# Attention, a routed expert layer and a second MLP on one core: a kernel's scheduler plans several times, with deadlines found backwards

## The chip, the core and the metric

The kernel runs on one core of one Trainium2 chip. The metric is the device time of one execution in microseconds (us), the median of several runs. The core has five engines with a queue each: TensorE (PE in the profile), VectorE (DVE), ScalarE (ACT), GpSimd (POOL) and SyncE (SP). SP issues most of the loads.

## The reference

Three layers follow one another. All inputs are float32.

```
scores = scale * q @ k^T             # B=4, H=8, S=576, D=64
scores = where(block_i >= block_j, scores, -1e9)      # blocks of 64
attn   = softmax(scores) @ v
x      = attn as [2304, 512]
...
logits = normalise(x) @ normalise(expert_emb)^T / tau   # 8 experts
e      = argmax(logits); gate_w = softmax(logits)[e]
x2[t]  = gate_w[t] * (relu(x[t] @ w1[e]) @ w2[e])     # 512 -> 1024 -> 512
...
h      = x2 @ w_in                                    # 512 -> 2048
out    = (h * sigmoid(h)) @ w_out                     # 2048 -> 512
```

## The kernel before

**Three stages.** Attention goes over 16 pairs (a batch and two heads). For each pair TensorE makes scores, DVE their row maxima, ACT the exponentials p, TensorE turns p by a matmul with the identity (pt) and multiplies it by v. Two things lie beside attention: the conversion of the second MLP's weights, and, as soon as the first 13 columns of 128 tokens are done, the routing of those tokens.

The expert layer goes over tiles of 128 tokens. A tile `s` holds tokens of one expert: its rows are gathered, turned (xt, L1297), multiplied by w1 (h, `first` L1315), sent through relu (L1331), turned again (ht, L1338), multiplied by w2 (y, `second` L1354) and scaled by the gate value (`yout`, L1377). There are 20 such tiles, and code behind a branch (`further`, L1524) for the case that more are needed.

The second MLP goes over chunks of three tiles: yt turns the rows, g multiplies by w_in, the silu follows (sg), o multiplies by w_out (`chunk`, L1390). Tiles and chunks are interleaved, so that the chunks give TensorE work from tile 3 on.

**Precision.** A product is made of three matmuls on a high and a low part of each operand. So weights are split on the way: ACT or DVE makes the high part (a CAST, w1s or w2s or w), DVE the low part (a subtraction). For the first tiles some of the four parts of the inner dimension are left whole and go through a plain float32 matmul: `DIRECT = (2, 1, 1, 1)` parts of tiles 0 to 3 (L47). The weights w_in and w_out arrive in a bit format that `_Convert` (L474) mends: 32 pieces of 512 KB (16 of w_in, 16 of w_out), each with one load, two ACT instructions and three or four of DVE. The last addition of pieces 0 to 11 is made on POOL, that of the rest on DVE. `CONV_AT` (L1610) says which of attention's pairs takes a piece along: 1 to 12. The other pieces follow between the tiles (`conv.more`).

**Who sets the order.** Nothing is written in its final order by hand. `_Plan` (L83) records every operation as an item: the engines that can do it, a cost in ns, what it depends on, and a rank, which is its place in the program plus a shift. `issue` (L350) then goes through time: at each step the engine that can begin first takes, among its items that are ready, the one with the smallest rank; a change of TensorE between float32 and float32r counts as 30 ranks (`STAY`). Where an item can go on two engines, the planner takes the one on which it ends sooner. A load's cost is its bytes at 360 B/ns (180 for runs under 512 bytes). What comes out are five fixed queues. The planner's costs decide only the order; on the chip each engine waits for what it really needs.

**Routing** is in three parts. `early` (L1089) finds the tokens of tiles 0 to 5 from the first 13 columns. `late` (L1121) chooses the experts of the other columns, and finds places and tokens (r_rows, r_tok_rhs and the tok matmuls) of tiles 6 on and the table of experts (esi). `rest` (L1144) makes the gate values (g1 for tiles 0 to 5, g2 for the rest). The squares of x, which the gate values need, are made by ACT at the end of attention (L869) into a ring of three PSUM buffers that attention's pt matmuls also use.

**Loads of weights.** `weights` (L1212) loads parts of an expert's w1 and w2 into wraw, a buffer that holds one expert; `begin` (L1242) starts the first tile's, in the order 0, 1, 2, 3.

All of it is recorded by one helper, so nearly every row of the profile has the line L192; rows are told apart by tile names. The functions that the change touches, and those that call them, are these:

Of the kernel before, what the change touches and what calls it, by code (L numbers as in the profile page):

```python
# [9 lines left out]
F32 = mybir.dt.float32  # L10
# [34 lines left out]
BG, WC, LM = 1, 2.4, 0.0  # L45
SM, CVS, SPS, ES = 0, 0, 40, 0
# [4 lines left out]
EARLY1, EARLY = 11, 26  # L51
# [7 lines left out]
STAY, CHANGE = 30, 190.0  # L59
SQS = 100  # L60
LS = -1000
# [21 lines left out]
class _Plan:  # L83
# [13 lines left out]
    class _Pool:  # L97
        def __init__(self, plan, pool, bufs):
            self.plan, self.pool, self.bufs = plan, pool, bufs
            self.names, self.done = [], set()  # L100
# [5 lines left out]
        def tile(self, shape, dt, tag=None, name=None, bufs=None):  # L106
# [5 lines left out]
            if tag is not None:  # L112
                ring = self.plan.rings.setdefault((id(self), tag), [])
# [8 lines left out]
    def __init__(self, tc):  # L122
        self.nc = tc.nc
        for e in self.ENGINES:
            setattr(self, e, self._Engine(self, e))
        self.rings, self.before, self.seen, self.users = {}, {}, {}, {}
# [8 lines left out]
        self.even = BW  # L135

# [62 lines left out]
    def call(self, alts, ins, outs, table=None, lead=0.0, dma=False):  # L199
# [3 lines left out]
        last = self.items[-1] if n and self.end[-1] is None else None  # L203
        pe = alts.get("tensor")
        if (pe and last is not None and "tensor" in last["alts"]
                and last["out"] == outs[0][0] and last["prio"] == n - 1 + self.shift
# [5 lines left out]
        else:  # L212
            it = dict(alts=alts, out=outs[0][0], deps=set(), table=table, lead=lead, dma=dma,
                      prio=n + self.shift, margin=self.margin if pe else 0.0)
# [77 lines left out]
    def _cost(self, engine, method, args, kw):  # L292
# [12 lines left out]
        if method == "dma_start":  # L305
# [4 lines left out]
            return n * mybir.dt.size(out.dtype) / (360.0 if run >= 512 else 180.0)  # L310
# [39 lines left out]
    def issue(self, ahead=100.0, until=()):  # L350


        items, free = self.items, self.free
        new = [n for n, end in enumerate(self.end) if end is None]
# [37 lines left out]
        while until:  # L392
            t, e = min((max(free[e], min(ready[n] for _, n in w)), e)
                       for e, w in waiting.items() if w)

            prio, n = min((x for x in waiting[e] if ready[x[1]] <= t + ahead),
                          key=lambda x: (x[0] + STAY * self._changes(e, items[x[1]]), x[1]))
# [21 lines left out]
            if it["dma"]:  # L419
# [6 lines left out]
                end = self.dma + 1150.0  # L426
# [23 lines left out]
    QUEUE = 1500.0  # L450

# [72 lines left out]
def _attention(first, ctx, late, tc, plan, q, k, v, emb, tau, x_dram, identr, lr_all, ss_all, conv=None):  # L524
# [85 lines left out]
    rmat = cp.tile([P, NPAIR, 2, D + E], F32, name="rmat")  # L610

# [201 lines left out]
    def e_units(i):  # L813
# [110 lines left out]
class _Route:  # L924
# [196 lines left out]
    def late(self, pool, psum):  # L1121
# [3 lines left out]
        self.choose(pool, NC1, NT)  # L1125
# [18 lines left out]
    def rest(self, pool, psum):  # L1144
# [24 lines left out]
        V.tensor_tensor(self.cpos[:, NE:], cp, dif, ALU.add)  # L1169


# [18 lines left out]
        for name, (rows, cols), m, s0 in (("g1", self.first, NC1, 0),  # L1190
                                          ("g2", self.second, NT, NE)):
            pt = self.invert(pool, psum, name, rows, cols, g3[:, 0:m])
            g = self.gate[:, s0:s0 + cols.shape[2]]
            V.tensor_copy(g, pt[:, 0])
            V.tensor_tensor(g, g, pt[:, 1], ALU.add)
            V.tensor_tensor(g, g, pt[:, 2], ALU.add)


def _layers(ctx, stage, early, scores, late, tc, plan, w1, w2, x_dram, y_dram, out, ident, route, xgs, conv, right):
# [12 lines left out]
    def weights(s, i, n, keep):  # L1212
# [4 lines left out]
        def f(eng):  # L1217
# [7 lines left out]
            else:  # L1225
# [7 lines left out]
                  [plan._box(wraw[:, i:i + n])], lead=1100.0 + 1000.0 * new, dma=True)  # L1233
# [8 lines left out]
    def begin(s, n=KC):  # L1242
        for i in range(0, 2 * KC, n):
            weights(s, i, n, False)
# [52 lines left out]
    def xt(s):  # L1297
        xg = XT[s]
        pt = psum(f"xt_{s}")
# [6 lines left out]
        ps["t"].close(pt)  # L1306
# [8 lines left out]
    def first(s, kc):  # L1315
        if kc == 0:
            HS[s] = [psum(f"h{n}_{s}") for n in range(2)]
        k = slice(kc * P, kc * P + P)
        if kc < direct(s):
            for n in range(2):  # L1320
                nc.tensor.matmul(HS[s][n], WH[s, "x"][:, k],
                                 wraw[:, kc, 512 * n:512 * n + 512], start=(kc == 0), stop=False)
# [3 lines left out]
        xh, xl = (XT[s][:, a, k] for a in range(2))  # L1326
        for n in range(2):
            c = slice(512 * n, 512 * n + 512)
            three(HS[s][n], xh, xl, hi[:, 0, c], lo[:, 0, c], kc == 0, kc == KC - 1)

    def relu(s):  # L1331
        h = htp.tile([P, FF], F32, tag="h", name=f"h_{s}")
        for n in range(2):
# [4 lines left out]
    def ht(s, n):  # L1338
        if n == 0:
            HT[s] = htp.tile([P, 2, FF], F32R, tag="ht", name=f"ht_{s}")  # L1340
        pt = psum(f"ht{n}_{s}")
# [8 lines left out]
        ps["t"].close(pt)  # L1350
# [3 lines left out]
    def second(s, i):  # L1354
        if i == 0:
            YP[s] = psum(f"y_{s}")
# [377 lines left out]
```

## Time and profile before

| | |
|---|---|
| runs | 911.73, 913.6, 916.29 us; median 913.6 us |
| the profiled execution | 912.01 us, span 910.3 us |
| granted TensorE clock, mean | 0.992 |
| instructions in the span | 13872 |

The profile is one execution on the chip. PE is TensorE's matmuls, PEld its weight loads, SPq is SP's queue. "Busy" leaves out waits on semaphores. An arrow `<-` after a duration in brackets names what ended the wait before the row's instruction; an `<-` between names stands between what is written and what is read. PEclk is the granted clock as a share of 2.4 GHz.

### The profile page before, as it was taken

To read this page: it belongs to the slowest core of one execution; us is meant where nothing else is said; L and a number is where in the kernel's file an instruction comes from. 1 tells how busy PE (TensorE), PEld (TensorE's weight loads), DVE (VectorE), ACT (ScalarE), POOL (GpSimd) and SP (SyncE) were. 2 spreads that over 40 slices of the span, in tenths; PEclk is the share of its full clock that TensorE was granted. 3 is DMA by queue.
4 is the path that set the end of the run, shared out by engine and by line. 5 is a ranking of instruction groups with operands and counts; after the bars stand their busy time and mean duration, and the time that the engine had idled before them with its cause. 6 is when DMAs were issued, how large, how long until landed. Compare 5 with 4: busy or idle time off the path is not lost.

```text
span 910.3 us, 13872 instructions
## 1 busy us (share of the span) xinstructions
PE 861.3 (95%) x4986; PEld 714.7 (79%) x4986; DVE 720.4 (79%) x1249; ACT 564.7 (62%) x1147; POOL 116.7 (13%) x158
## 2 busy tenths in 40 slices
PE   5999999987899989999999999999999999999995
PEld 4777677655567878887888888888898998898894
DVE  5889899776889979999788888888667667666672
ACT  6888787766468658879766566676334334334332
POOL 2112121224100000012311110031001001001001
PEclk9999999999899999999999999999999999999998
DMA  5436353352133338751200322143102002000000
GB/s 186 138 114 173 104 180 97 76 208 64 62 139 133 131 106 281 269 185 42 71 24 24 116 68 72 58 139 105 58 1 70 1 1 70 1 0 36 1 1 35
DMA packets 38441, 82.77 MB, mean 91 GB/s; under 512 B 5208, under 2 KB 13400, under 8 KB 38368
## 3 DMA queue, kind: packets, MB, share of 16 engines
q1 hardware_dynamic: 32736, 63.47, 21.1%
q0 software_dynamic: 5632, 18.36, 6.5%
q8 instruction: 41, 0.67, 0.3%
q14 instruction: 32, 0.26, 0.1%
HBM read 123.23 MB, written 13.11 MB: 150 GB/s over the span
## 4 chain that ended last, share of the span: by engine, by line
PE 61%; issue 0%; DVE 0%; ACT 0%; POOL 0%; POOLq 0%; ACTq 0%
PE o L192 20%; PE g L192 20%; PE y L192 9%; PE h L192 9%; PE ht L192 1%; PE yt L192 1%; PE xt L192 1%; POOL out_dram L1465 0%; ACT ys L192 0%; POOLq L1729 0%; DVE sg L192 0%; DVE ht L192 0%; ACT sg L192 0%; DVE yt L192 0%; DVE xt L192 0%
## 5 line engine op out<-in xcount | busy, mean ns | idle before, releaser
L192 PE MATMUL o<-w,g 128*128 128x512 f32 x864 | 228.5, 396 | 0.0
L192 PE MATMUL g<-yt,w 128*128 128x384 f32 x1152 | 227.5, 338 | 0.2 <-issue 0.2
L192 PEld LDWEIGHTS g<-yt,w 128*128 128x128 f32 x1152 | 203.2, 188 | 13.5 <-issue 0.5
L192 PEld LDWEIGHTS o<-w,g 128*128 128x128 f32 x864 | 160.5, 188 | 30.4 <-DVE g L192 0.7
L192 ACT ACTIVATE sg<-g 128x384 f32<-128x384 f32 x96 | 47.3, 493 | 136.2 <-PE g L192 135.6
L192 PE MATMUL y<-w2s,ht 128*128 128x512 f32 x450 | 128.8, 400 | 0.7 <-DVE w2s L192 0.7
L192 PE MATMUL h<-w1s,xt 128*128 128x512 f32 x450 | 112.3, 400 | 0.7 <-ACT xt L192 0.5
L192 DVE TENSOR_TENSOR w1s<-wraw,w1s 128x1024 fp32r<-128x1024 f32 x75 | 91.4, 1222 | 18.6 <-ACT w1s L192 18.0
L192 PEld LDWEIGHTS h<-w1s,xt 128*128 128x128 f32 x450 | 84.5, 189 | 22.0 <-issue 2.7
L192 DVE TENSOR_TENSOR w2s<-wraw,w2s 128x1024 fp32r<-128x1024 f32 x75 | 91.2, 1223 | 11.9 <-ACT w2s L192 10.0
L192 PEld LDWEIGHTS y<-w2s,ht 128*128 128x128 f32 x450 | 81.1, 188 | 13.7 <-DVE w2s L192 1.0
L192 ACT ACTIVATE p<-s,mx 128x576 f32<-128x576 f32 (+4 forms) x160 | 82.1, 524 | 12.6 <-DVE mx L192 12.0
L192 ACT CAST w2s<-wraw 128x1024 fp32r<-128x1024 f32 x67 | 70.6, 1054 | 23.4 <-PE y L192 8.3
L192 DVE TENSOR_REDUCE mx<-s 128x1 f32<-128x576 f32 (+2 forms) x96 | 64.8, 705 | 17.1 <-PE s L250 16.7
L192 DVE TENSOR_TENSOR w<-win,w 128x512 fp32r<-128x512 f32 x96 | 65.8, 688 | 15.8 <-ACT w L192 15.6
L192 ACT CAST g<-sg 128x384 fp32r<-128x384 f32 x96 | 49.3, 515 | 43.9 <-DVE sg L192 42.4
L192 ACT CAST w1s<-wraw 128x1024 fp32r<-128x1024 f32 x59 | 62.3, 1058 | 21.0 <-PE y L192 10.0
L250 PE MATMUL s<-ks,qs 64*128 64x288 f32 (+4 forms) x576 | 60.0, 341 | 12.8 <-ACT p L192 6.4
L192 DVE TENSOR_TENSOR w<-wout,w 128x512 fp32r<-128x512 f32 x96 | 65.6, 684 | 1.8 <-ACT w L192 1.6
L192 ACT CAST w<-win 128x512 fp32r<-128x512 f32 x87 | 54.0, 623 | 19.8 <-PE o L192 19.5
L192 PE MATMUL pt<-ident,p 128*128 128x128 f32 (+1 forms) x400 | 60.4, 287 | 5.8 <-ACT p L192 2.2
L250 PEld LDWEIGHTS s<-ks,qs 64*128 64x128 f32 x576 | 46.5, 198 | 18.9 <-ACT p L192 9.3
(192 smaller groups left out, 1110.5 us busy)
## 6 DMA issues: line engine op xcount, KB each, us to landing
wraw<-in_moe_w_dram SPq DMA_DIRECT2D x76, 1024.0 KB
wbits<-in_moe_w_in_dram SPq DMA_DIRECT2D x16, 512.0 KB
wbits<-in_moe_w_out_dram SPq DMA_DIRECT2D x16, 512.0 KB
k<-in_k_dram SPq DMA_DIRECT2D x16, 288.0 KB
q<-in_q_dram SPq DMA_DIRECT2D x16, 288.0 KB
v<-in_v_dram SPq DMA_DIRECT2D x16, 256.0 KB
x_rows<-xe POOLq DMA_DIRECT2D x16, 256.0 KB, 4.9
wraw<-in_moe_w_dram SPq DMA_DIRECT2D x8, 512.0 KB
```

Of the source, the lines that this page charges most:

```text
L192: alts = {e: (lambda eng, m=m, a=a, k=k: getattr(eng, m)(*a, **k), self._cost(e, m, a, k), self._shares(e, m, a, k) if e != "tensor" else ...
L250: eng.matmul(out, a, b, **kw)
```

## The change

The instructions that compute stay nearly the same in kind and number; their order and in some places their engine change.

- **Several plans.** `_best` builds the kernel four times (`ROUNDS = 3`). After each build `latest` goes backwards through the plan and finds the latest start of each item that still keeps the plan's length; this start is the item's rank in the next build. The plan that is shortest by the planner's own costs is kept. `STAY` becomes 2000 ns in these builds.
- **Costs.** A load's bytes go at 250 B/ns (165 for runs under 2048 bytes), and weights are taken to be ready 2500 ns later (`WL`).
- **Order of the inner parts.** `ORD = (2, 3, 1, 0)`: the split parts of a tile's inner dimension come first and the whole ones last, and the loads follow. The two halves of h are turned in the order 1, 0.
- **Squares** are written into an SBUF tile `sqs` instead of the PSUM ring.
- **Gate values.** `gates` is new and stands ahead of `late`: the choice of experts for the other columns, the gate values and g1. g2 follows in `rest`.
- **Conversion.** `CONV_AT` goes from -1 to 14 (16 pieces) instead of 1 to 12, and `conv.more` begins behind tile 2 instead of behind tile 0.
- yr gets a pool of its own, and the first program part of tiles reaches to `ready[2]` instead of unit 26.

```
-STAY, CHANGE = 30, 190.0
+STAY, STAY_NS, CHANGE = 30, 2000.0, 190.0
+ROUNDS = 3
+ORD = (2, 3, 1, 0)
+WL = 2500.0
...
-            return n * mybir.dt.size(out.dtype) / (360.0 if run >= 512 else 180.0)
+            return n * mybir.dt.size(out.dtype) / (250.0 if run >= 2048 else 165.0)
...
+            it["prio"] = self.order[n] if self.order else n + self.shift
...
-                          key=lambda x: (x[0] + STAY * self._changes(e, items[x[1]]), x[1]))
+                          key=lambda x: (x[0] + self.stay * self._changes(e, items[x[1]]), x[1]))
...
-                end = self.dma + 1150.0
+                end = self.dma + 1150.0 + it["late"]
...
+    def latest(self):
...
+        free = dict.fromkeys(self.ENGINES, self.length())
+        due = dict.fromkeys(live, self.length())
...
+        for _ in live:
+            t, e = max((min(free[e], max(w)[0]), e) for e, w in waiting.items() if w)
+            x = max((x for x in waiting[e] if x[0] >= t - 100.0), key=lambda x: (x[1], x[3]))
+            waiting[e].remove(x)
+            n = x[3]
+            free[e] = order[n] = min(free[e], x[0]) - x[2]
...
+            for m in items[n]["deps"]:
+                if m in after:
+                    due[m] = min(due[m], order[n] - items[n]["margin"])
...
+def _best(build):
+
+    nc, plan = build(None)
+    last = plan
+    for _ in range(ROUNDS):
+        found, last = build(last.latest())
+        if last.length() < plan.length():
+            nc, plan = found, last
+    return nc
...
-            sq = ps_t.tile([P, H, D], F32, tag="t", name=f"sq{tl}_{i}")
             plan.shift = SQS
-            nc.scalar.activation(sq[a:e], (XE[b][a:e, tl] if tl < 4 else x4[a:e])[:, :, 0:D],
+            nc.scalar.activation(sqs[a:e], (XE[b][a:e, tl] if tl < 4 else x4[a:e])[:, :, 0:D],
...
     def late(self, pool, psum):
-        self.choose(pool, NC1, NT)
...
+    def gates(self, pool, psum):
+        self.part = 4
+        self.choose(pool, NC1, NT)
...
+        self.places_of(pool, psum, "g1", self.first, NC1, 0)
...
-        for i in range(0, 2 * KC, n):
-            weights(s, i, n, False)
+        for h in range(2):
+            for i in ORD if n == 1 else range(0, KC, n):
+                weights(s, KC * h + i, n, False)
...
-                for kc in range(KC):
+                for kc in ORD:
                     add(1.3, first, s, kc)
...
-                for i in range(KC):
+                for i in ORD:
                     add(1.3, second, s - 1, i)
...
-                for _ in range(more if s else 0):
+                for _ in range(more if s > 2 else 0):
                     add(0.0, conv.more)
...
-CONV_AT = {i: 1 for i in range(1, 13)}
+CONV_AT = {i: 1 for i in range(-1, 15)}
```

What this does to the queues is shown at three places. In a row, the instruction writes what stands left of the arrow and reads what stands right of it; x4 counts several in a row.

**The first instructions of ScalarE.** esq is the square of the experts' embedding, qs_i and ks_i are pair i's q and k in float32r, p_0 the first exponentials. Before:

```order
L192 ACTIVATE esq_137,en_s_138<-em_135 8x512
L192 ACTIVATE qs_0_142<-q_0_129 128x576
L192 ACT_TABLE_LOAD
L192 ACTIVATE en_s_138<-en_s_138 8x1
L192 CAST ks_1_149<-k_1_139 128x576
L192 ACT_TABLE_LOAD
L192 ACTIVATE en_s_138<-en_s_138 8x1
L192 ACTIVATE qs_1_150<-q_1_140 128x576
L192 CAST ks_2_166<-k_2_146 128x576
L192 ACTIVATE p_0_151,rs_132<-s40_0_152,mx_0_4_0_154 128x576
```

Now:

```order
L199 CAST ks_0_142<-k_0_128 128x576
L199 ACTIVATE qs_0_143<-q_0_129 128x576
L199 ACTIVATE esq_138,en_s_139<-em_136 8x512
L199 CAST ks_1_150<-k_1_140 128x576
L199 ACT_TABLE_LOAD
L199 ACTIVATE en_s_139<-en_s_139 8x1
L199 ACT_TABLE_LOAD
L199 ACTIVATE en_s_139<-en_s_139 8x1
L199 ACTIVATE p_0_152,rs_132<-s40_0_153,mx_0_4_0_155 128x576
```

The first pair's q and k come ahead of esq, k is converted on ACT instead of DVE, and qs_1 and ks_2 now stand behind the first exponentials.

**TensorE between tile 0 and tile 1.** xt, h, ht and y are the steps of a tile, with the tile's number last; tok is the routing's tokens of tiles 6 on (17 rows of one kind in the queue, one of them shown), ptot its first matmul. Before:

```order
L192 MATMUL xt_1_2875<-ident_62,xg_72 128x128 x4
L192 MATMUL ht0_0_3088<-ident_62,h_0_3086 128x128 x4
L192 MATMUL ht1_0_3090<-ident_62,h_0_3086 128x128 x4
...
L192 MATMUL tok_3066<-r2_tok_rhs_3065,r2_rows_3063 128x38
L192 MATMUL h0_1_3091<-wraw_2438,x32_1_2877 128x512
L192 MATMUL h1_1_3092<-wraw_2438,x32_1_2877 128x512
L192 MATMUL y_0_3096<-wraw_2438,h32_0_3089 128x512 x2
```

Now:

```order
L199 MATMUL xt_1_2928<-ident_62,xg_72 128x128 x4
...
L199 MATMUL ptot_3085<-r_oh_267,c_ones_260 128x144
L199 MATMUL ht1_0_3112<-ident_62,h_0_3110 128x128 x4
L199 MATMUL ht0_0_3113<-ident_62,h_0_3110 128x128 x4
L199 MATMUL h0_1_3115<-w1s_1_2_3117,xt_1_2929 128x512 x3
L199 MATMUL h1_1_3116<-w1s_1_2_3117,xt_1_2929 128x512 x3
...
L199 MATMUL xt_3_3141<-ident_62,xg_72 128x128 x4
...
L199 MATMUL tok_3096<-r2_tok_rhs_3095,r2_rows_3093 128x38
```

The tok matmuls have moved from straight behind tile 0's ht to behind tile 3's xt; tile 1's h begins with split weights straight behind ht.

**SP's queue at the change from attention to the tiles.** v_15 is attention's last load, esi the table of experts, wraw the first tile's weights, wbits the pieces for the conversion. Before:

```order
L192 DMA v_14_597<-in_v_dram 128x512
L192 DMA v_15_649<-in_v_dram 128x512
L1239 TENSOR_LOAD esi_67
L1239 ISA x2
L1224 ISA
L1224 DMA wraw_2438<-in_moe_w1_dram 128x1024
```

Now:

```order
L199 DMA v_15_641<-in_v_dram 128x512
L199 DMA wbits_14_639<-in_moe2_w_in_dram 128x4x256
L1328 TENSOR_LOAD esi_67
L1328 ISA x2
L1312 ISA
L1312 DMA wraw_2419<-in_moe_w1_dram 128x1024
...
L1312 DMA wraw_2419<-in_moe_w1_dram 128x1024
L199 DMA wbits_15_668<-in_moe2_w_in_dram 128x4x256
L1316 ISA
L1316 DMA wraw_2419<-in_moe_w2_dram 128x2x512
```

A piece for the conversion stands ahead of the read of esi, which the weights' addresses come from, and another between the first tile's w1 and w2.

## Rows read from the trace of the kernel before

**Rows 1.** The page: busy time of each engine.
```profile
PE 861.3 (95%) x4986; PEld 714.7 (79%) x4986; DVE 720.4 (79%) x1249; ACT 564.7 (62%) x1147; POOL 116.7 (13%) x158
```

**Rows 2.** Busy time by stretch; columns as in the first row (us from the start).
```profile
core 0: us, PE busy (x) PEld busy (x) DVE busy (x) ACT busy (x) POOL busy (x), PEclk, DMA share, GB/s
0.00:25.00 25.00, 14.81 (x88) 12.20 (x90) 15.82 (x43) 17.66 (x42) 6.71 (x36) 1.00 0.58 182
25.00:175.00 150.00, 143.67 (x1298) 106.98 (x1299) 131.09 (x269) 122.05 (x375) 27.52 (x25) 1.00 0.41 124
175.00:212.00 37.00, 31.17 (x278) 22.43 (x277) 26.30 (x80) 22.94 (x68) 7.88 (x9) 1.00 0.49 160
212.00:281.00 69.00, 57.02 (x268) 38.26 (x267) 59.97 (x125) 43.28 (x73) 12.54 (x11) 0.93 0.35 109
226.20:233.00 6.80, 6.05 (x25) 2.88 (x26) 6.80 (x22) 0.34 (x2) 1.52 (x1) 0.50 0.15 41
...
281.00:328.00 47.00, 46.16 (x227) 39.50 (x226) 43.73 (x73) 32.76 (x56) 0.94 (x1) 1.00 0.28 96
...
350.00:425.00 75.00, 74.32 (x367) 62.94 (x367) 72.41 (x104) 62.91 (x97) 6.34 (x7) 1.00 0.59 198
425.00:650.00 225.00, 224.94 (x1116) 192.60 (x1115) 186.57 (x233) 148.79 (x224) 35.89 (x42) 1.00 0.21 71
...
900.00:910.30 10.30, 1.05 (x5) 0.52 (x3) 0.00 (x0) 0.88 (x2) 3.32 (x5) 0.76 0.20 76
```

**Rows 3.** What TensorE waited for: us in total, times, longest.
```profile
PE s L250 <- ACT p L192: 6.4, 6, 2.5
PE s L250 <- ACT qs L192: 6.0, 1, 6.0
PE tok L192 <- DVE r_tok_rhs L192: 5.1, 1, 5.1
PE xt L192 <- PEq L1529: 2.9, 1, 2.9
```

**Rows 4.** Order of time on ScalarE, start: start us, us, instruction, [idle before <-releaser].
```profile
4.63 0.63 ACT L192 ACTIVATE esq<-em 8x512 f32<-8x512 f32 x1 [2.54 <-DMA em<-in_moe_expert_emb_dram]
...
5.26 0.67 ACT L192 ACTIVATE qs<-q 128x576 fp32r<-128x576 f32 x1
...
10.87 0.73 ACT L192 ACTIVATE p<-s,mx 128x576 f32<-128x576 f32 x1
```

**Rows 5.** The same on VectorE, start.
```profile
3.80 0.46 DVE L192 CAST ks<-k 128x576 fp32r<-128x576 f32 x1 [1.62 <-DMA k<-in_k_dram]
```

**Rows 6.** Order of time on TensorE, tiles 0 to 2.
```profile
226.95 0.75 PE L192 MATMUL tok<-r_tok_rhs,r_rows 128*128 128x38 bf16 x18 [5.15 <-DVE r_tok_rhs L192]
...
248.97 1.12 PE L192 MATMUL h<-wraw,x 128*128 128x512 f32 x2 [2.11 <-DVE xt L192]
...
264.88 0.66 PE L192 MATMUL xt<-ident,xg 128*128 128x128 f32 x4 [1.42 <-ACT yr L192]
```

**Rows 7.** Groups on VectorE by form: busy us, mean ns, then idle before them.
```profile
L192 DVE SCALAR_TENSOR_TENSOR wcv<-wbits,wcv 128x512 int32<-128x512 int32 x32 | 21.9, 686 | 0.3
...
L192 DVE TENSOR_SCALAR wcv<-wcv 128x512 f32<-128x512 f32 x32 | 13.8, 431 | 1.7 <-ACT wcv L192 1.7
...
L192 DVE TENSOR_SCALAR wcv<-wcv 128x512 int32<-128x512 int32 x32 | 13.5, 421 | 0.2
...
L192 DVE CUSTOM_DVE_ANT_0 wout<-wbits,wcv 128x1024 uint16<-128x1024 uint16 x16 | 11.0, 688 | 0.6
L192 DVE CAST w1s<-wraw 128x1024 fp32r<-128x1024 f32 x16 | 11.0, 686 | 4.6 <-PEq L1529 4.2 <-PE y L192 0.4
```

**Rows 8.** Groups on ScalarE by form.
```profile
L192 ACT CAST w<-win 128x512 fp32r<-128x512 f32 x87 | 54.0, 623 | 19.8 <-PE o L192 19.5 <-DVE win L192 0.3
...
L192 ACT ACTIVATE sq<-xe 128x512 f32<-128x512 f32 x16 | 9.6, 597 | 1.6 <-DVE xe L192 1.2 <-DVE x L192 0.4
```

**Rows 9.** What SyncE's queue waited for: us in total, times, longest.
```profile
SPq L192 <- DVE wout L192: 36.7, 10, 7.0
```

More of the change, by code (lines that the diff above doesn't have):

```diff
@@ L112, in tile @@
             if tag is not None:
[L113 removed]
+                ring = self.rings.setdefault(tag, [])
                 n = bufs or self.bufs
@@ L135, in __init__ @@
         self.even = BW
+        self.stay = STAY_NS if order else STAY
     def pool(self, pool, bufs):
@@ L353, in issue @@
         items, free = self.items, self.free
+        self.fence = len(items)
+        for n in until:
+            items[n].setdefault("fence", self.fence)
         new = [n for n, end in enumerate(self.end) if end is None]
@@ L450, with length, put @@
     QUEUE = 1500.0
+    def length(self):
+        return max(self.free.values())
+    def latest(self):
+        items = self.items
+        live = [n for n in range(len(items)) if self.end[n]]
+        after = {n: [] for n in live}
+        for n in live:
+            for m in items[n]["deps"]:
+                if m in after:
+                    after[m].append(n)
+        free = dict.fromkeys(self.ENGINES, self.length())
+        due = dict.fromkeys(live, self.length())
+        left = {n: len(after[n]) for n in live}
+        order = [float(it["rank"]) for it in items]
+        waiting = {e: [] for e in self.ENGINES}
+        later, held = {}, {}
+        for n in live:
+            it = items[n]
+            if "fence" in it:
+                later[it["fence"], it["engine"]] = 0
+        for f, e in later:
+            later[f, e] = sum(items[n]["engine"] == e for n in live if n >= f)
+        def put(n):
+            it = items[n]
+            f = it.get("fence"), it["engine"]
+            if later.get(f):
+                held.setdefault(f, []).append(n)
+                return
+            e, cost = it["engine"], it["alts"][it["engine"]][1]
+            if not it["dma"]:
+                takes, lag = cost, self.LATENCY[e]
+            elif e == "gpsimd":
+                takes, lag = 1040.0, 1860.0 + it["late"]
+            else:
+                takes = max(cost, 580.0, it["lead"] + 60.0)
+                lag = 1730.0 + it["late"] + cost + it["lead"] - takes
+            waiting[e].append((due[n] - lag, self.end[n], takes, n))
+        for n in live:
+            if not left[n]:
+                put(n)
+        for _ in live:
[4 more added lines that the diff above has]
+            free[e] = order[n] = min(free[e], x[0]) - x[2]
+            for f in later:
+                if f[1] == e and n >= f[0]:
+                    later[f] -= 1
+                    if not later[f]:
+                        for m in held.pop(f, ()):
+                            put(m)
+            for m in items[n]["deps"]:
+                if m in after:
+                    due[m] = min(due[m], order[n] - items[n]["margin"])
+                    left[m] -= 1
+                    if not left[m]:
+                        put(m)
+        return order
@@ L1189, in rest, with places_of @@
                 V.tensor_tensor(gt, gt, g3[:, :, a], ALU.subtract)
[L1190 to L1196, printed above, removed]
+        self.g3 = g3
+        self.places_of(pool, psum, "g1", self.first, NC1, 0)
+    def places_of(self, pool, psum, name, found, m, s0):
+        V = self.nc.vector
+        rows, cols = found
+        pt = self.invert(pool, psum, name, rows, cols, self.g3[:, 0:m])
+        g = self.gate[:, s0:s0 + cols.shape[2]]
+        V.tensor_copy(g, pt[:, 0])
+        V.tensor_tensor(g, g, pt[:, 1], ALU.add)
+        V.tensor_tensor(g, g, pt[:, 2], ALU.add)
 def _layers(ctx, stage, early, scores, late, tc, plan, w1, w2, x_dram, y_dram, out, ident, route, xgs, conv, right):
@@ L1232, in weights @@
         plan.call({"sync": (f, 600.0 * n * (1 if keep else WC))}, ins,
-                  [plan._box(wraw[:, i:i + n])], lead=1100.0 + 1000.0 * new, dma=True)
+                  [plan._box(wraw[:, i:i + n])], lead=1100.0 + 1000.0 * new, dma=True,
+                  late=WL)
     REG = {}
@@ L1495, in load @@
         def load(s, i):
-            if s < end and (i + 1) % LG == 0:
-                weights(s, i + 1 - LG, LG, keep)
+            if s < end and i % KC in ORD[1::2]:
+                weights(s, i // LG * LG, LG, keep)
         for s in range(lo, hi + 1):
@@ L1519, in tiles @@
                 add(0.0, relu, s)
-                for n in range(2):
+                for n in (1, 0):
                     add(0.45, ht, s, n)
@@ L1567, in _layers @@
         routing = range(n, len(plan.items))
-        for _, f in seq_s[EARLY1:EARLY]:
+        early = ready[2]
+        for _, f in seq_s[EARLY1:early]:
             f()
@@ L1623, in tile_kernel @@
 @with_exitstack
-def tile_kernel(ctx, tc, q, k, v, emb, tau, w1, w2, w_in, w_out, out):
+def tile_kernel(ctx, tc, q, k, v, emb, tau, w1, w2, w_in, w_out, out, order=None):
     nc = tc.nc
@@ L1636, in tile_kernel @@
     y_dram = dr.tile([NTOK - NE * P + P, DM + 1], F32, name="y_rows")
-    plan = _Plan(tc)
+    plan = _Plan(tc, order)
     xgs = cp.tile([P, 2, DM], F32, name="xg")
```

90 lines of the change are left out of this document (52 added, 38 removed).

## The prediction

> **What bounds the kernel now.** I read the profile's totals first. TensorE is busy for 861.3 of 910.3 us, DVE for 720.4 [rows 1]. So the program is TensorE's, and only its idle 49 us and whatever it does at a low clock can be won by another order. The windows say where these are [rows 2]. From 425 to 650 TensorE is busy for 224.94 of 225 us: nothing to win there, and I take the stretches behind it as alike up to the last ten, where it is busy for 1.05 us (the last output's way out, which the change doesn't touch). The idle time stands ahead of 281: 10.2 us in the first 25, 6.3 from 25 to 175, 5.8 from 175 to 212, 12.0 from 212 to 281, and 0.8 from there to 328. In 212 to 281 the granted clock is 0.93 as well, and in 226.2 to 233 it is 0.50, which is 1.2 GHz. In that stage DVE is busy for 59.97 of 69 us and TensorE for 57.02, the latter partly at half clock: here DVE is the fuller engine.
>
> The waits say what TensorE stood for [rows 3]: the scores' PSUM buffers, until the exponentials had been made (6 waits, 6.4 us), the first qs (6.0), one wait of 5.1 us of the routing's tok matmuls for r_tok_rhs from DVE, and 2.9 us at the branch for more tiles. In order of time [rows 6] the 5.15 us before tok, at 226.95, come first; the clock of 0.50 lies around them, and then come 2.11 us for xt from DVE and 1.42 for yr from ACT.
>
> **The start.** ACT did esq at 4.63, qs at 5.26 for 0.67, and the first exponential at 10.87 [rows 4]. DVE had k at 3.80 [rows 5]. In the new order ACT makes ks and qs first: 3.80 plus two instructions of this shape, 0.67 each, is 5.14, where scores could begin at 5.93 before, if q has landed by then (qs waited for nothing but esq, so the rows don't show when it came). That is -0.8. For the first exponential the ACT chain loses qs_1 and ks_2, gains ks_0 and begins 0.83 earlier: -0.83 + 0.67 - 1.34 = -1.5. I take **-1.2**, bounds -0.5 to -2.
>
> **Attention, 25 to 212.** Two edits meet here. The squares leave the PSUM ring that pt matmuls use, and the latest starts order the queues; what they could give at most is TensorE's idle time, 6.3 + 5.8 = 12.1 us. Against that, four more pieces are converted here, and pieces past the twelfth have all their steps on DVE: 431 + 421 + 686 + 688 ns [rows 7], 2.23 us each, 8.9 us in all. DVE was busy for 131.09 + 26.30 us of 187 [rows 2], so 29.6 us stand free for them, but it is DVE that makes the maxima and ACT the exponentials that TensorE waits for. Bounds: -6, half of the idle time, and +5, about half of the added DVE work on the path. ACT is busy for 145 of 187 us and has room. I take **-2**, nearer to the gain, since the free time is more than three times what is added.
>
> The squares themselves took 597 ns each into PSUM, and a CAST of 128x512 from SBUF into SBUF took 623 [rows 8]. For the 16 of this size and 4 smaller ones the new place costs 20 x 0.026 = 0.5 us of ACT by these rows, on an engine with 42 us to spare: nothing in the sum. The Trainium skill speaks against the edit (ScalarE: Activation LUTs, section "Step-by-step: what each stage is for"): of the two places to write to, PSUM is the nearer for ScalarE, but only worth it while TensorE doesn't need the space. If all of it fell on the path, the attention term would be -1.5 instead of -2; here TensorE does want the ring, so I keep -2.
>
> **Tiles 0 to 3, 212 to 281.** DVE's work here shrinks. Counted in the built queues between the subtractions of xt_0 and xt_4, conversion pieces fall from 5 to 2 (-3 x 2.23 = -6.7), the chunks' weight subtractions from 3 to 2 (-0.69), and high parts of expert weights that DVE rather than ACT makes rise from 4 to 8 (+4 x 0.686 = +2.7, by the CAST w1s, [rows 7]). The sum is -4.6 of 59.97. TensorE's queue no longer stands for the tok matmuls behind tile 0's ht; they come behind tile 3's xt, and h of tile 1 takes their place with split weights. So the 5.15 us should go. What is late next there is DVE: its queue has the two CASTs and subtractions of w1s for tile 1 ahead of xt_1 and ht_0. If DVE's idle 9.0 us remain, the stage gives just its work, 69.0 - 4.6 = 64.4. If the waits that made DVE idle go with it down to 3 us, it takes 59.97 - 4.6 + 3 = 58.4. I take the middle, **-7.6**, bounds -3 and -12.
>
> In the first of these the half clock needn't go: 0.93 of 69 us means about 4.8 us without clock pulses, and a fall like it stays if another wait of this length comes. The Trainium skill (TensorE: Matmul & The Clock Gate, section "HAM oscillation — how this bites in real kernels") says that waits which come again each time let the clock fall each time. By it the stage would win nothing of the clock while a wait for DVE stands at each tile; the rows show one such fall, at the one long wait. That is the second rival below.
>
> **Behind tile 3.** Four g steps of chunk 0 move from before the branch to behind it. They are TensorE's work on either side: 0. From 350 to 425 DVE is busy for 72.41 of 75 us and TensorE for 74.32 [rows 2], so there DVE is nearly full beside a full TensorE; two more pieces fall behind the branch (10 to 12), 2 x 2.23 = 4.5 us of DVE. If they land in that stretch, up to 4.5 is TensorE's loss; later, where DVE is busy for 186.57 of 225, they are hidden. I take **+1**, bounds 0 and +4.5. The 2.9 us of the branch and the end stay.
>
> **The sum** is -1.2 - 2 - 7.6 + 1 = -9.8 against the profiled execution of 912.0: 902.2, say **902**. That execution is 1.6 us under the median of 913.6, and the difference lies within the spread of the runs (911.73 to 916.29), so I don't correct for it. With not every bound at its end at once, the forecast's own range is 893 to 908.
>
> **Rival 1: everything runs at TensorE's pace.** The backward plan makes the waits vanish and not just the one. Then attention gives 9 of its 12.1 idle us, the tiles' stage 14 (its idle 12.0 and half of the clock's 4.8), the start 1.2: 912 - 24 = 888. For it: DVE has room in attention. Against it: attention's waits come from the chain scores, maxima, exponentials with its few PSUM buffers [rows 3], which no order lengthens, and DVE would have to be full in the tiles' stage. 0.13.
>
> **Rival 2: the waits move.** The planner's costs find a shorter plan, the chip has other durations. DVE remains the fuller engine in the tiles' stage, TensorE stands for w1s or xt at each of four tiles where it stood once for tok, and the clock falls there; attention pays for its four pieces with +3. With the start: 912 - 1.2 + 3 - 3 + 1 = 912, and 909 to 915 around it. For it: a DVE CAST stands ahead of xt_1 and ht_0. 0.14. That the change doesn't do what it says belongs here too: if the kept plan is hardly better than the first.
>
> **Rival 3, slower: SP's queue.** A conversion's load waits for its staging buffer, in order, and all behind it waits as well. That wait took 36.7 us in 10 times, 3.7 each and 7.0 at the longest [rows 9]. Now one stands ahead of the read of esi, one between the first tile's w1 and w2, and pairs stand among the weights of tiles 3, 4 and those behind the branch, on a buffer that holds one expert. If the expert's weights then come too late at five tiles, the price is 5 x 3.7 = 18.5, and 912 - 9.8 + 18.5 = 921. It decides from the point where 3.7 us is more than the time by which weights lie ready before their split. Against it: the first piece's load waits for pieces that DVE has converted long before, and the planner now counts weights as late by 2.5 us and leaves them more time. 0.09.
>
> **How the numbers follow.** The forecast has 0.64, the rivals 0.13, 0.14 and 0.09. A measurement of this kernel tells about 0.5%, 4.6 us, from no change: faster means under 909.0, slower over 918.2. Faster: the forecast's 0.62 and rival 1's 0.13, 0.75. Same: 0.02 of the forecast, rival 2 nearly whole, a little of rival 3, 0.16. Slower: 0.09. The range for 8 in 10 leaves out half of rival 1 and most of rival 3 and reaches past rival 2's middle: **888 to 914**.
>
> **What would show it right or wrong.** Right: TensorE has no wait for r_tok_rhs, the stage from the first xt to the turning of tile 3's h takes under 64 us at a clock near 1.00, and the first scores begin at about 5.1 us. TensorE's idle time in 25 to 212 falls from 12.1 to about 10. Wrong in attention: that idle time rises, with waits for p or mx. Wrong in the stage: new waits for w1s, xt or ht from DVE add up to more than 9 us, or the clock there is again under 0.95. Wrong behind it: TensorE's idle time from 281 to 650 rises above 3 us, or wraw waits show in the chain. A time over 914 or under 888 makes the whole account wrong.

## The result and the profile after

| | before | the change |
|---|---|---|
| runs, median | 914.94 us (911.73 to 916.82, 4 runs) | 892.32 us (891.71 to 893.46, 4 runs) |
| ratio, 95% interval | | 0.9758 (0.9725 to 0.979) |
| the profiled execution's span | 910.3 us | 890.4 us |

The change is faster by 2.1 to 2.75%: 19.9 us between the two profiled spans. The forecast was 902 with a range of 888 to 914; 892.3 lies in the range, but the gain is twice what was forecast, and it lies just under the forecast's own 893.

Busy time of each engine after the change, against [rows 1]:

```profile
PE 856.0 (96%) x4986; PEld 713.9 (80%) x4986; DVE 722.6 (81%) x1264; ACT 554.1 (62%) x1128; POOL 121.9 (14%) x162
```

TensorE does the same 4986 matmuls. Of 19.9 us, 5.3 went from its busy time and 14.6 from its idle time. Some 3 of the 5.3 are the clock: 4.8 us without clock pulses from 212 to 281 before, 1.7 from 190 to 193.5 now. The rest isn't accounted for. The same stretches as in [rows 2], and two short ones:

```profile
core 0: us, PE busy (x) PEld busy (x) DVE busy (x) ACT busy (x) POOL busy (x), PEclk, DMA share, GB/s
0.00:25.00 25.00, 14.81 (x95) 12.43 (x97) 17.46 (x44) 18.26 (x43) 8.53 (x37) 1.00 0.63 189
25.00:175.00 150.00, 144.90 (x1312) 107.62 (x1310) 132.65 (x281) 124.89 (x382) 29.88 (x28) 1.00 0.46 135
175.00:212.00 37.00, 35.24 (x282) 26.49 (x283) 31.92 (x91) 26.61 (x76) 8.18 (x10) 0.95 0.55 181
185.00:190.00 5.00, 3.59 (x47) 3.21 (x44) 4.80 (x16) 3.62 (x9) 2.31 (x4) 1.00 0.93 350
190.00:193.50 3.50, 3.50 (x24) 3.32 (x24) 3.23 (x8) 1.44 (x5) 1.19 (x2) 0.52 0.68 221
212.00:281.00 69.00, 62.33 (x307) 43.33 (x306) 65.82 (x126) 44.71 (x71) 14.19 (x11) 1.00 0.33 106
281.00:328.00 47.00, 45.61 (x223) 38.52 (x222) 41.75 (x59) 31.85 (x50) 2.12 (x3) 1.00 0.52 177
350.00:425.00 75.00, 75.00 (x377) 64.36 (x376) 70.51 (x102) 62.21 (x98) 13.14 (x13) 1.00 0.35 113
425.00:650.00 225.00, 225.00 (x1121) 193.85 (x1121) 182.17 (x241) 136.64 (x214) 29.36 (x37) 1.00 0.22 71
```

Between 25 and 212 TensorE idles for 6.9 us, where it idled for 12.1. Between 212 and 281 it idles for 6.7 instead of 12.0, and its clock is 1.00 instead of 0.93. From 350 to 650 it doesn't idle at all. DVE is busy for 65.82 of 69 us in the tiles' stage: it is now nearly full there. What TensorE waited for, against [rows 3]:

```profile
PE s L258 <- ACT p L199: 7.7, 6, 3.6
PE s L258 <- ACT qs L199: 5.3, 1, 5.3
PE h L199 <- DVE xt L199: 2.0, 2, 1.8
PE xt L199 <- DVEq L1623: 1.4, 1, 1.4
...
PE xt L199 <- ACT yr L199: 0.8, 1, 0.8
...
PE tok L199 <- DVE r_tok_rhs L199: 0.4, 1, 0.4
```

The wait for r_tok_rhs has shrunk from 5.1 to 0.4 us and the one at the branch (xt, for PEq or DVEq) from 2.9 to 1.4; the scores wait about as before.

**Two landmarks.** The stretches above hold different work in the two kernels. So I measure between the same two instructions: DVE's subtraction for xt of tile 0, where the tiles' stage begins, and that of tile 4. Before, in order of time:

```profile
213.77 0.68 DVE L192 TENSOR_TENSOR xt<-xt,xt 128x512 fp32r<-128x512 f32 x1
...
283.50 0.68 DVE L192 TENSOR_TENSOR xt<-xt,xt 128x512 fp32r<-128x512 f32 x1
```

After:

```profile
206.02 0.69 DVE L199 TENSOR_TENSOR xt<-xt,xt 128x512 fp32r<-128x512 f32 x1
...
267.63 0.69 DVE L199 TENSOR_TENSOR xt<-xt,xt 128x512 fp32r<-128x512 f32 x1 [0.26 <-ACT xt L199]
```

These cut the span in three parts. Up to xt_0: 213.8 and 206.0, 7.8 us less. From xt_0 to xt_4: 69.7 and 61.6, 8.1 less. From xt_4 to the end: 910.3 - 283.5 = 626.8 and 890.4 - 267.6 = 622.8, 4.0 less. The sum is 19.9. The cut at xt_0 isn't clean. TensorE's last matmuls for attention (e) end at 213.9 before and at 209.6 now:

```profile
212.39 1.49 PE L192 MATMUL e<-rmat,ot 128*128 128x144 f32 x10
```

```profile
208.16 1.39 PE L199 MATMUL e<-rmat,ot 128*128 128x144 f32 x10
```

By this mark attention ends 4.3 us earlier and not 7.8, and what lies from there to xt_4 is 11.5 us shorter. The first part is flattered by matmuls that the second now carries; only the sum up to xt_4, 15.9, doesn't depend on the mark.

### The profile page after: what moved, and what is told of

The parts are those of the page before. It is cut to its first block, busy times and chain, and to the rows that moved or that the text cites. A ratio compares the mean times of both kernels' runs of the same rounds, so it can differ in the third digit from the quotient of the medians.

```text
span 890.4 us, 13848 instructions
## 1 busy us (share of the span) xinstructions
PE 856.0 (96%) x4986; PEld 713.9 (80%) x4986; DVE 722.6 (81%) x1264; ACT 554.1 (62%) x1128; POOL 121.9 (14%) x162
## 4 chain that ended last, share of the span: by engine, by line
PE 65%; POOL 0%; POOLq 0%; issue 0%; ACT 0%
PE o L199 22%; PE g L199 22%; PE y L199 9%; PE h L199 9%; PE ht L199 2%; PE xt L199 1%; PE yt L199 1%; POOL out_dram L1559 0%; POOLq L1838 0%; ACT os L199 0%; POOL ix L1558 0%; POOLq L1559 0%
## 5 line engine op out<-in xcount | busy, mean ns | idle before, releaser
L199 PE MATMUL o<-w,g 128*128 128x512 f32 x864 | 234.2, 396 | 0.0
L199 PE MATMUL g<-yt,w 128*128 128x384 f32 x1152 | 230.7, 337 | 0.0
L199 PE MATMUL y<-w2s,ht 128*128 128x512 f32 x450 | 131.3, 402 | 1.2 <-DVE w2s L199 1.2
L199 PE MATMUL h<-w1s,xt 128*128 128x512 f32 x450 | 110.4, 394 | 3.4 <-DVE xt L199 2.0
L199 PEld LDWEIGHTS y<-w2s,ht 128*128 128x128 f32 x450 | 81.2, 188 | 16.3 <-DVE w2s L199 2.7
L258 PE MATMUL s<-ks,qs 64*128 64x288 f32 (+4 forms) x576 | 61.3, 344 | 13.1 <-ACT p L199 7.7
L199 DVE TENSOR_REDUCE mx<-s 128x1 f32<-128x576 f32 (+3 forms) x96 | 64.6, 705 | 10.5 <-PE s L258 9.5
L199 ACT CAST w1s<-wraw 128x1024 fp32r<-128x1024 f32 x53 | 55.6, 1054 | 20.7 <-PE y L199 15.2
L199 ACT CAST w<-win 128x512 fp32r<-128x512 f32 x75 | 46.6, 625 | 28.7 <-PE o L199 28.6
L199 DVE TENSOR_TENSOR sg<-g,sg 128x384 f32<-128x384 f32 x96 | 53.3, 556 | 10.6 <-ACT sg L199 7.9
```

Source lines behind the costliest of these rows:

```text
L199: alts = {e: (lambda eng, m=m, a=a, k=k: getattr(eng, m)(*a, **k), self._cost(e, m, a, k), self._shares(e, m, a, k) if e != "tensor" else ...
L258: eng.matmul(out, a, b, **kw)
```

## The experiments

Every kernel here does the whole computation. The landmarks of each were read as above; they come from one profiled execution each, while the ratio comes from all timed runs against runs of the kernel before on the same chip.

| kernel | median us | ratio (95%) | to xt_0 | xt_0 to xt_4 | xt_4 to end |
|---|---|---|---|---|---|
| before | 914.9 to 917.0 | 1 | 213.8 | 69.7 | 626.8 |
| the change | 892.3 | 0.9758 (0.9725 to 0.979) | 206.0 | 61.6 | 622.8 |
| e1 first plan | 919.7 | 1.003 (0.9999 to 1.0061) | 219.5 | 61.5 | 631.0 |
| e2 deadlines only | 912.1 | 0.9946 (0.9929 to 0.9962) | 219.1 | 63.1 | 627.2 |
| e3 gates last | 895.4 | 0.977 (0.9739 to 0.9801) | 207.5 | 62.8 | 623.3 |
| e4 squares in PSUM | 902.7 | 0.9846 (0.9815 to 0.9877) | 215.3 | 62.0 | 623.5 |
| e5 conversion 12 | 905.4 | 0.9894 (0.9854 to 0.9933) | 213.1 | 62.3 | 626.8 |
| e6 inner order | 901.5 | 0.9857 (0.9813 to 0.9902) | 214.9 | 60.5 | 622.9 |
| e7 load costs | 907.3 | 0.9908 (0.9872 to 0.9943) | 218.8 | 61.3 | 624.7 |
| e8 deadlines, squares | 904.5 | 0.9895 (0.9862 to 0.9928) | 208.6 | 64.0 | 626.7 |
| e9 plan 1 | 900.5 | 0.9814 (0.9787 to 0.984) | 214.7 | 59.4 | 626.1 |
| e10 plan 2 | 906.8 | 0.9886 (0.9862 to 0.991) | 223.5 | 60.4 | 622.8 |
| e11 ranks shaken | 901.3 | 0.9821 (0.9794 to 0.9847) | 217.7 | 59.4 | 622.8 |
| e12 more whole parts | 899.8 | 0.9821 (0.9794 to 0.9848) | 209.2 | 60.1 | 628.3 |

In e3, e4, e6 and e12 too, some of attention's matmuls stand behind xt_0; the two columns ahead of xt_4 are then safer read as a sum.

### The deadlines or the edits?

**e1**, the change without its deadlines:

```
-ROUNDS = 3
+ROUNDS = 0
```

> The change with its first plan only (no deadlines; every other edit stays). Theory D (the deadlines give the gain): 907 to 915 us, at most a third of the 22 us are left, and TensorE waits 4 us or more in all at the end of attention (177 to 200). Theory E (the edits to the program give it, above all the gate values set apart and the squares off the ring): 893 to 900 us, with no wait of over 2 us in the tiles' stage.

It gains nothing: 1.003. The profiled execution, 913.7 us, is among its fastest. Its tiles' stage is as short as the change's (61.5 us), but it begins 5.7 us later than before and the rest is 4.2 us longer. The clock has a part in that: it is 0.97 from 25 to xt_0, where it was 1.00 before. The landmarks:

```profile
219.47 0.68 DVE L199 TENSOR_TENSOR xt<-xt,xt 128x512 fp32r<-128x512 f32 x1
...
280.96 0.68 DVE L199 TENSOR_TENSOR xt<-xt,xt 128x512 fp32r<-128x512 f32 x1
```

Its waits, all through the program:

```profile
PE pt L199 <- ACT p L199: 3.8, 8, 0.9
PE o L258 <- DVE pt L199: 3.2, 4, 1.4
PE h L199 <- ACT xt L199: 2.0, 3, 1.1
PE h L199 <- DVE w1s L199: 2.0, 1, 2.0
PE yt L199 <- DVE yt L199: 1.9, 3, 1.2
```

The tok matmuls behind tile 0 no longer wait for r_tok_rhs there either, without any deadline; what replaces it are many waits of about 1 us, in attention (pt, o) and in the tiles and chunks (h, yt).

**e2**, the kernel before with the several plans alone (the rest of the diff undone):

```
-            it = dict(..., prio=n + self.shift, ...)
+            it["prio"] = self.order[n] if self.order else n + self.shift
...
+    for _ in range(ROUNDS):
+        found, last = build(last.latest())
```

> The kernel before, with the several plans and nothing else of the change (old DMA costs, squares in PSUM, gate values last, 12 pieces over attention, inner parts in the order 0 to 3). Theory D: 895 to 903 us, the wait of 5.15 us for r_tok_rhs gone. Theory E: 909 to 915 us, and that wait still there at 3 us or more.

0.5% faster. Theory D had asked for 895 to 903. The wait is shorter, not gone:

```profile
PE s L258 <- ACT p L199: 8.8, 7, 5.0
...
PE xt L199 <- PEq L1618: 2.8, 1, 2.8
...
PE tok L199 <- DVE r_tok_rhs L199: 2.1, 1, 2.1
```

Its tiles' stage is 6.6 us shorter than before, but xt_0 comes 5.3 us later, so that up to xt_4 only 1.3 us are won. DVE still has the five pieces of conversion there:

```profile
219.11:282.17 63.06, 52.94 (x254) 35.12 (x253) 57.51 (x122) 44.98 (x73) 11.24 (x10) 0.97 0.40 124
```

So both theories, as I put them, fell: the edits alone give nothing, the deadlines alone 0.5%, both together 2.4%. e1 and e2 are one plan each; another plan of e2 was not measured.

### Undoing one edit at a time

**e3**, the choice of experts and the gate values back in their old place:

```
-        route.gates(r, lambda name: psum(name, "c"))
...
     def late(self, pool, psum):
+        self.choose(pool, NC1, NT)
```

> The change with the choice of the later columns' experts and the gate values back in their old place in the program (everything else stays, planned again). Theory D: within 3 us of the change, 889 to 896 us. Theory E: the wait for r_tok_rhs comes back, with the clock's fall 6 to 10 us: 898 to 903 us.

The same as the change: the intervals of the two ratios cover each other nearly whole, and the tiles' stage of 62.8 us has no wait for r_tok_rhs. The gate values' place is worth nothing that shows in this one plan.

**e4**, the squares back in the ring:

```
-            nc.scalar.activation(sqs[a:e], ...
+            sq = ps_t.tile([P, H, D], F32, tag="t", name=f"sq{tl}_{i}")
+            nc.scalar.activation(sq[a:e], ...
```

> The change with the squares back in the ring of PSUM buffers of the pt matmuls (everything else stays, planned again). Theory D: within 3 us of the change, 889 to 896 us. Theory E: 896 to 900 us, all of it lost between 175 and 212 as waits of pt matmuls for ScalarE.

902.7 us, above Theory E's range; some 8 us are lost by the ratios, all of it ahead of xt_0 (215.3 against 206.0), about where Theory E had put it. But the waits that it named, of pt for ScalarE between 175 and 212, come to 0.9 us there.

**e5**, twelve pieces over attention again:

```
-CONV_AT = {i: 1 for i in range(-1, 15)}
+CONV_AT = {i: 1 for i in range(1, 13)}
...
-                for _ in range(more if s > 2 else 0):
+                for _ in range(more + (s < 7) if s > 2 else 0):
```

> The change with 12 pieces over attention at pairs 1 to 12, and the four others two to a tile behind tile 3 (still none behind tiles 1 and 2). Theory S (each edit frees a few us for the deadlines; the sum is spread): 893 to 898 us, attention 1 to 3 us shorter than in the change since DVE has 8.9 us less there, and 2 to 5 us more lost behind tile 3, where DVE is nearly full. Theory W (one edit, the squares, is what the deadlines needed): within 2 us of the change.

905.4 us, and not where expected: attention has less to do and yet xt_0 comes 7.1 us later than in the change. Behind xt_4 it loses 4.0 us, as expected, 2.1 of them at the branch, where the wait is 3.5 us against the change's 1.4:

```profile
PE xt L199 <- DVEq L1623: 3.5, 1, 3.5
PE y L199 <- DVE w2s L199: 2.3, 3, 1.1
```

**e6**, the inner parts in their old order:

```
-ORD = (2, 3, 1, 0)
+ORD = (0, 1, 2, 3)
```

(relu and the turning of h with it.)

> The change with the inner parts in the order 0 to 3 again, loads, relu and the turning of h with them. Theory S: 895 to 901 us, lost between 212 and 281 because the first tiles' whole parts come first and hold PE at h until xt's whole part is copied. Theory W: within 2 us of the change.

901.5 us, half a us above the range that Theory S gave, and lost in another place: the tiles' stage is 60.5 us, shorter than the change's, and xt_0 comes 8.9 us later. The edit touches no line of attention.

**e7**, the old costs of a load:

```
-            return n * mybir.dt.size(out.dtype) / (250.0 if run >= 2048 else 165.0)
+            return n * mybir.dt.size(out.dtype) / (360.0 if run >= 512 else 180.0)
...
-WL = 2500.0
+WL = 0.0
```

> The change with the old costs of a load (360 and 180 B/ns, weights not counted as late). Theory S: 895 to 901 us, with TensorE waiting for DVE's w1s and w2s between 212 and 425 for 3 us or more, as weights come later than planned. Theory W: within 2 us of the change.

907.3 us, worse than either theory said, and again with the loss ahead of xt_0 (218.8) while the tiles' stage is as in the change (61.3). The waits for DVE's w1s and w2s that Theory S named come to 1.5 us in all.

**e8**, the deadlines and the squares in SBUF, nothing else:

```
-            sq = ps_t.tile([P, H, D], F32, tag="t", name=f"sq{tl}_{i}")
+            nc.scalar.activation(sqs[a:e], ...
```

> The kernel before with the several plans and the squares in SBUF, nothing else of the change. Theory W: 895 to 903 us, since the squares are what the deadlines needed. Theory S: 904 to 910 us, some 4 to 8 us under the deadlines alone and all of that in attention, while the tiles' stage stays as it was with the deadlines alone.

904.5 us, where Theory S put it; the profiled execution is among its fastest. Against e2 all of the gain lies ahead of xt_0 (208.6 against 219.1; by the ratios it is 5 us).

The five single reverts (e3 to e7) cost 1 to 14 us by their ratios, and in four of them (e4 to e7) xt_0 is 7 to 13 us later, though e6 changes no operation of attention, and e7 only what the planner takes a load to cost. That pointed to another reading: each edit makes the scheduler plan anew, and a new plan gives attention another order. A single revert then shows the edit and a draw of the plan together.

### The same program, other plans

**e9** keeps the second of the change's four plans, **e10** the third; **e11** moves every deadline by a random amount (normal, 100 ns) and keeps the third:

```
-ROUNDS = 3
+ROUNDS = 1
```

```
-ROUNDS = 3
+ROUNDS = 2
...
-        if last.length() < plan.length():
-            nc, plan = found, last
+        nc, plan = found, last
```

```
-        found, last = build(last.latest())
+        found, last = build([x + rng.gauss(0.0, 100.0) for x in last.latest()])
```

> The change, every edit in, but the second of its four plans kept (one step of deadlines; by the planner's own costs 5.4 us longer than the kept one). Theory L (what the chip gives follows the plan's own length, whatever the edits, so part of the gain is that this plan is the shortest of several): 895 to 901 us. Theory S (the edits with any plan by deadlines give it): 890 to 895 us. Theory Q (plans are a draw, and the planner's length tells nothing of the chip): anywhere from 890 to 910, out of the order of lengths.

> The change, every edit in, with the third plan kept (by the planner's own costs 9.0 us longer than the kept one, the longest of the three by deadlines). Theory L: 898 to 905 us, and longer than with the second plan. Theory S: 890 to 895 us. Theory Q: out of the order of lengths.

> The change, every edit in, with each deadline moved by a random 100 ns (normal), the third plan kept; by the planner's own costs it is 3.1 us longer than the change. Theory L: 893 to 899 us. Theory S: 890 to 895 us. Theory Q: anywhere from 890 to 910. In each case the loss, if any, stands ahead of tile 4, in attention too, which no edit of this run names.

The same edits with three other plans by deadlines give 0.9814, 0.9886 and 0.9821, where the change gives 0.9758. Theory S (890 to 895) falls in all three. In e10 the loss is ahead of xt_0:

```profile
223.49 0.69 DVE L199 TENSOR_TENSOR xt<-xt,xt 128x512 fp32r<-128x512 f32 x1 [0.65 <-ACT xt L199]
...
283.93 0.69 DVE L199 TENSOR_TENSOR xt<-xt,xt 128x512 fp32r<-128x512 f32 x1 [0.25 <-ACT xt L199]
```

and its waits from 25 to 215 are many of about 1 us behind ScalarE and DVE:

```profile
PE pt L199 <- ACT p L199: 4.6, 8, 1.0
PE s L258 <- ACT p L199: 2.7, 5, 1.0
PE pt L199 <- ACT pt L199: 2.2, 3, 1.4
```

From 25 to xt_0 TensorE is idle for 15.1 us, against 6.9 in the change, and its clock is 0.97; one of its falls, at 0.50, covers 205.5 to 212:

```profile
25.00:223.49 198.49, 183.40 (x1582) 133.05 (x1583) 164.61 (x366) 149.75 (x450) 35.96 (x34) 0.97 0.44 132
```

Between plans of one program xt_0 comes at 206.0, 214.7, 217.7 and 223.5, a spread of 17.5 us about the 213.8 of before (14.4 by the end of the last e, 16.3 up to xt_4). The stage behind it takes 59.4 to 61.6, and the rest 622.8 to 626.1. So what the change gains ahead of xt_0 belongs to this plan; what it gains in the tiles' stage comes with every one of these plans, though in e10 the later xt_0 takes it all back: xt_4 is at 283.9, against 283.5 before. All four are faster than e2, the slowest at 0.9886 (0.9862 to 0.991) against 0.9946 (0.9929 to 0.9962). It also means that the costs of the single reverts e4 to e7, 8 to 14 us, are hardly larger than what a new plan alone does (5 to 12 us by the ratios), and that none of them shows what its edit is worth.

Theory L did better than the others: by the planner's own costs the four plans are longer in the order change, e11 (+3.1), e9 (+5.4), e10 (+9.0); by the ratios times 915 they are longer by 5.8, 5.1 and 11.7 us. The longest is the longest on the chip; e9 and e11 can't be told apart. In us e10 and e11 lie about 2 above the range given, since the kernel before took 916.9 beside them.

**e12**, a version meant to beat both:

```
-DIRECT = (2, 1, 1, 1)
+DIRECT = (2, 2, 2, 1)
```

> A version that may beat both: the change with two whole parts for tiles 1 and 2 and one for tile 3 (DIRECT = (2, 2, 2, 1)), so that DVE and ACT split two parts of w1 and of w2 less ahead of tile 4; the planner's own length is 2.8 us shorter. Theory L: 887 to 892 us. Theory that DVE bounds the tiles' stage: 886 to 891 us, DVE less busy there by up to 4 x 1.9 us. If TensorE bounds the stage now: 891 to 896 us, since a whole part goes through TensorE in four passes where the split one takes three.

899.8 us, above every range given, though by the planner it is the shortest. The tiles' stage is 1.5 us shorter, xt_0 is 3.2 later and the rest 5.5 longer. In the stage DVE is busy for 51.75 us, 4.6 less than in the change, for those 1.5 us:

```profile
209.16:269.23 60.07, 54.58 (x267) 34.96 (x263) 51.75 (x114) 36.10 (x61) 17.37 (x13) 1.00 0.31 95
```

So DVE's work alone doesn't set the stage's time. TensorE's waits between 270 and 350, around which the clock is 0.53 from 304 to 311:

```profile
PE xt L199 <- DVEq L1623: 2.6, 1, 2.6
PE xt L199 <- issue: 1.5, 1, 1.5
```

So the planner's length ordered the plans of one program, but not this edit of it. No run here beat the change.

## Why the prediction was right, and where it was wrong

**What bounds: right.** Nearly the whole gain lies in TensorE's idle time ahead of 360 and in its clock, and the steady stretch from 425 on didn't move (225.00 of 225 busy).

**The start, -1.2: nearly right.** ACT's first rows, against [rows 4]:

```profile
3.84 0.67 ACT L199 CAST ks<-k 128x576 fp32r<-128x576 f32 x1 [1.75 <-DMA k<-in_k_dram]
4.54 0.68 ACT L199 ACTIVATE qs<-q 128x576 fp32r<-128x576 f32 x1
...
10.06 0.72 ACT L199 ACTIVATE p<-s,mx 128x576 f32<-128x576 f32 x1
```

qs ends at 5.22, where 5.14 was forecast; the first exponential is at 10.06 instead of 10.87, which is -0.8 and not -1.5. The wait for qs went from 6.0 to 5.3.

**Attention, -2: the step that failed.** With the start, 3.2 us were forecast ahead of xt_0; the change shows 7.8, or 4.3 by the end of attention's last matmul, which lies within the bounds. The number is not where the step failed. The step priced the edits (squares off the ring, four more pieces on DVE) as if each had a cost of its own in a fixed order. e9 to e11 have the same edits and begin the tiles' stage at 214.7, 223.5 and 217.7: the term isn't a cost of the edits, but what a given plan does with 16 pairs of short chains. e10 is 9.7 us later than before, past the bound of +5, and that the change came out on the good side is this plan's luck as far as the forecast goes, or the choice of the shortest plan, which the step didn't price. It should have been carried as a spread of some 14 to 17 us, which is wider than the bounds of -6 and +5. DVE had more to do in 25 to 212, 164.57 us against 157.39 (in the change the last 6 us of that stretch belong to the tiles), and TensorE's idle time fell all the same.

**The squares.** They take 638 ns into SBUF against 597 into PSUM [rows 8]:

```profile
L199 ACT ACTIVATE sqs<-xe 128x512 f32<-128x512 f32 x16 | 10.2, 638 | 1.6 <-DVE xe L199 1.4
```

That is 41 ns more each where 26 was taken: 0.8 us of ACT in place of 0.5, beside other work. The rule of the Trainium skill cited in the prediction (ScalarE: Activation LUTs, section "Step-by-step: what each stage is for") agrees in its direction. Whether the ring was worth it isn't shown: e4 loses 8 us and e8 gains 5 against e2 by the ratios, both ahead of xt_0, both no more than other plans differ.

**Tiles 0 to 3, -7.6: right in time, -8.1; the mechanism is only in part shown.** The window between the two landmarks shows the terms. Before:

```profile
213.77:283.50 69.73, 56.95 (x259) 37.53 (x259) 61.39 (x127) 45.07 (x76) 12.54 (x11) 0.93 0.36 115
```

After:

```profile
206.02:267.63 61.61, 54.96 (x281) 36.89 (x277) 56.30 (x116) 36.21 (x61) 16.58 (x13) 1.00 0.29 89
```

DVE's work fell by 5.1 us (4.6 forecast) and its idle time from 8.3 to 5.3 (the middle between 9 and 3 was taken). The wait for r_tok_rhs is down to 0.4 us, and the clock no longer falls. What replaces it is the wait named, 1.79 us for xt from DVE at tile 1, around which the clock stayed at 1.00. What is not shown is that this takes the whole change: the first plan without deadlines has 61.5 us, and the deadlines without the edits 63.1, with 2.1 us of that wait left. Either does most of it. Nor did it take the term's largest part, three pieces of conversion fewer: e2 keeps all five and its stage is 6.6 us shorter, while e12 has 4.6 us less of DVE's work than the change for 1.5 us.

**The clock.** The forecast left open whether it would fall again at each tile's wait. It didn't: 1.00 from xt_0 to xt_4, and of the waits left there only that one is over 1 us. The prediction read one fall in the kernel before; there were two in this stage, the second at 0.51 from 250 to 253.4, behind the 2.11 us for xt (its row is in the last section). So rival 2 had more for it than was said. The rule of the Trainium skill cited in the prediction (TensorE: Matmul & The Clock Gate, section "HAM oscillation — how this bites in real kernels") isn't tried by the change, since the long waits themselves are gone. In the kernel before, the waits of 5.15 and 2.11 us were followed by a fall, those of 1.42 and 2.92 weren't.

**Behind tile 3, +1: wrong in sign, -4.0.** The DVE work that I put on the path was hidden: from 350 to 425 DVE is busy for 70.51 us, less than the 72.41 of before, since pieces now fall elsewhere. And two small things that I left at nothing were gains: the wait at the branch is 1.4 us in place of 2.9, and TensorE's waits of under a microsecond between 281 and 425 are gone (0.0 idle in 350 to 425 against 0.7). Every run with the edits and the deadlines except e5, e7, e9 and e12 has 622.8 to 623.5 here; the first plan has 631.0, with a fall of the clock to 0.50 from 314 to 316 in it. Which edit gives it isn't settled; the pool of its own for yr, which the forecast never priced, was not tried alone.

**The rivals.** Rival 1 (888) was nearer in time than the forecast, but not by its mechanism: TensorE still idles for 6.7 us between 212 and 281, with DVE nearly full, and the stage gave 8.1 and not 14. Rival 2 failed: the waits for DVE at the tiles stayed short and the clock didn't fall, and the kept plan (0.9758) is well ahead of the first (1.003). Rival 3 (SP's queue): the waits for DVE's wout shrank, against [rows 9], but those for POOL's win, the last step of w_in's first pieces, rose. Before:

```profile
SPq L192 <- POOL win L192: 17.7, 11, 5.4
```

After:

```profile
SPq L199 <- POOL win L199: 47.5, 12, 6.2
...
SPq L199 <- DVE wout L199: 16.4, 7, 5.2
```

In sum these waits didn't shrink (54.4 and 63.9 us). But no wait for a load is among TensorE's in the tiles' stage, so it cost nothing that shows there.

## What to carry to other kernels

Where a scheduler sets the order, the time of one plan isn't the worth of an edit: four plans of one program spread over 0.9758 to 0.9886, as much as undoing single edits did. Keeping the shortest of several plans paid here, and an edit is to be judged by several plans with it and several without; that was not done here for any edit. A stage in which one engine is nearly full came out near the price of its work (DVE: 4.6 forecast, 5.1 found), though e2 and e12 warn that this work doesn't alone set it; a stage of many short chains had no such price, and its term should be a spread.

## What the runs showed of the hardware

The clock fell without a long wait, and stayed up behind one. In the change it is 0.52 of full in 190 to 193.5, nearly all at 1.2 GHz, after 5 us in which TensorE was busy for 3.59 and waited 1.4 us at the longest (for p). In the kernel before TensorE was busy for less in a stretch like it, 3.00 of 5 us in 195 to 200, with 1.2 us as its longest wait, and the clock stayed at 2.4 GHz:

```profile
195.00:200.00 5.00, 3.00 (x34) 2.39 (x36) 4.08 (x13) 4.09 (x17) 2.29 (x2) 1.00 1.02 384
200.00:205.00 5.00, 5.00 (x40) 3.19 (x37) 3.27 (x5) 1.87 (x4) 0.00 (x0) 1.00 0.69 261
```

The fall in the change cost little: 0.48 of 3.5 us, 1.7 us without clock pulses. Elsewhere in the kernel before, the clock fell to 0.51 from 250 on, behind a wait of 2.11 us that ended at 248.97, and stayed at 1.00 around the wait of 2.92 us at the branch, which ended at 333.36:

```profile
250.00:253.40 3.40, 3.40 (x8) 1.98 (x7) 3.33 (x7) 1.25 (x2) 0.00 (x0) 0.51 0.60 214
...
328.00:335.00 7.00, 4.08 (x21) 3.13 (x20) 2.76 (x3) 2.56 (x4) 0.92 (x2) 1.00 0.40 142
```

So in these rows the length of the longest wait doesn't tell by itself which of them are followed by a fall.
